# Decayed keys of six blocks turned by DMA instead of TensorE, in a linear-attention kernel followed by a dense layer

## The chip, the cores and the metric

One core of a Trainium2 chip runs the whole program. The metric is the device time in microseconds of one execution. Before the change three runs took 573.35, 575.41 and 577.69 us, median 575.41 us.

## The reference

An RWKV-6 attention over batch 4, 8 heads, 768 tokens and head size 48, and then a dense layer whose activation is h - tanh(h):

```
for t in range(S):
    cur = einsum('bhd,bhe->bhde', u * k_t, v_t)
    y_t = einsum('bhd,bhde->bhe', r_t, state + cur)
    state = w_t[..., None] * state + einsum('bhd,bhe->bhde', k_t, v_t)
x = y as [3072, 384]
h = x @ w_in            # [3072, 2048]
out = (h - tanh(h)) @ w_out
```

All inputs and outputs are 32-bit floats.

## The kernel before, in words

The work is cut into eight blocks: 4 batches times 2 halves of 384 tokens. Block 0's attention is computed first (`boot`). Then the loop `for i, blk in enumerate(blocks)` runs the dense layer of block i in 16 steps (`f` from 0 to 15, 128 columns of the hidden layer each), and between the steps, on the same engines, the attention of the next block (`later`, block i+1) and the first preparations of the one after it (`after`, block i+2). "Step 7 of block 4" below means f = 7 in the loop for i = 4. Every engine's order of instructions is written out by hand (`manual_schedule`) and is the order in which the program emits them; an engine whose next instruction has to wait holds up everything behind it. SP issues nearly all DMAs, in one queue.

**A step of the dense layer.** TensorE (PE) makes `hp` by three matmuls (L720) into a single PSUM buffer, so the next step's `hp` can only start when ScalarE has copied this one to `h` (L723). From block 2 on ScalarE then does three more passes of 384 (L741, L742, L744), VectorE (DVE) makes `g` from them one step later (L726), and then forms sums of pieces of `g` (L767), which PE multiplies two steps later (L835): in these "fast" blocks the second product is done in pairs of steps with fewer products of 128x128. In blocks 0 and 1 the second product is the plain one (L797). A block takes about 66 us.

**The attention of the next block.** A tile holds two pairs of heads in each half (`HALVES` = pairs 2, 3 and pairs 0, 1; `UP` = 2); partitions are head dimensions, columns are tokens. DVE scans the decays `w` from behind into the tile `post` (`behind`, L387) and from the front into `pre` (`before`, L376), and multiplies keys into `post` (`times_behind`, L401) and r into `pre` (`times_before`, L394). `bound` (L418, ScalarE) reads `w` for a check. Then PE works through phases, each put at a step by `plan(i)`:

- `earlier`: products of `post` and `pre` (L447), copied under a mask by DVE (L454);
- `turn`: `post` has to be had with tokens on the partitions. PE transposes 12 pieces of 128x128 (L471) into two PSUM scratch tiles, and ScalarE copies them into the tile `ks` (L473, two copies of 768);
- `update`: PE multiplies `ks` with `v` (L496); one step later DVE chains the products into the states (`update_2`, L508 and L518, eleven or twelve instructions);
- `result 1` and `result 2`: PE multiplies states (L561) and scores (L578); ScalarE copies the result to `xT`, the input of the next block's dense layer.

Other DVE work of the next block, on keys and r with tokens on the partitions: `product_u` (L343), `product_r` (L347), `product_sum` (L351), `diagonal_in` (L358). The two token tables are loaded at steps 3 and 4 (L339; at 4 and 5 in block 1), into the tiles `k` and `r`; `w`, `k` and `r` of the block after are loaded at steps 7, 9 and 11 (L330) into the same tiles, each of which has one buffer. `post`, `w` and `ks` have one buffer too.

Of the kernel before, what the change touches and what calls it, by code (L numbers as in the profile page):

```python
# [42 lines left out]
U16 = mybir.dt.uint16  # L43
# [8 lines left out]
P = 128  # L52
L = 64
NB = 384
NQ = S // NB
NCH = NB // L
NCP = NCH // 2
# [3 lines left out]
HALF = WIDE // 2 + 2  # L61
UP = 2
# [58 lines left out]
def kernel(  # L121
# [12 lines left out]
    nc = tc.nc  # L134
# [29 lines left out]
    start = const.tile([P, UP * NCH * LP], F32, name="start", tag="start")  # L164
# [116 lines left out]
    class Block:  # L281
# [183 lines left out]
        def turn(self, ps, p0, ahead=0):  # L465
# [6 lines left out]
                                        self.chunk("post", p0 + p, 2 * c, n=2), ident)  # L472
            nc.scalar.copy(out=ks.rearrange("t p c d -> t p (c d)"), in_=tp[:, :, 0:NCP * P])  # L473

        def keys(self):
            if not hasattr(self, "ks"):
                self.ks = work.tile([P, NPAIR, NCP, P], F32, name="ks", tag="ks", bufs=1)
            return self.ks
# [142 lines left out]
        def phase(self, ps, name):  # L621

            if name in ("own", "earlier"):
                return [getattr(self, name)(ps, p0) for p0 in HALVES]
            if name == "turn":
                for p0 in HALVES:
                    self.turn(ps, p0)
            elif name == "update":
                self.update_1(ps)
                return [self.update_2]  # L630
            elif name == "result 1":
                self.results(ps)
                self.result("from_states", ALL)
            elif name == "result 2":
                self.result("from_scores", ALL, True)
                self.result_out(ALL)
                self.fill_holes([nc.sync])
            return []
# [247 lines left out]
    def plan(i):  # L886


        converted = ()
        if i == 0:  # L890
            phases = {4: "turn", 6: "update", 8: "own", 11: "earlier", 13: "result 1"}
            before = {0: ("behind 2", "take_whole 2"), 1: ("behind 0", "take_whole 0", "times_behind 2"),
                      2: ("times_behind 0",), 3: ("before 2",), 4: ("times_u 2",), 5: ("before 0", "times_u 0"),
                      8: ("times_before", "held", "bound 2"), 9: ("bound 0",)}
            ahead = {}
            converted = range(READY + 1, NF)
            loads = {f: "weights" for f in (0, 1, 3, 4, 5, 6, 7, 8, 9, 10)}
            loads.update({2: "next r", 11: "w", 12: "k", 13: "r"})
        else:
            phases = {4: "earlier", 7: "turn", 10: "update", 12: "result 1"}  # L900
            before = {0: ("times_behind 2",), 1: ("times_behind 0",), 3: ("times_before", "held"), 4: ("bound 2",),
                      5: ("product_u",), 6: ("bound 0", "product_r"), 7: ("product_sum",), 8: ("diagonal_in 2",),
                      9: ("diagonal_in 0",)}
            if i == 1:
                phases = {6: "earlier", 8: "turn", 10: "update", 12: "result 1"}
                before.update({0: ("behind 2", "take_whole 2"), 1: ("behind 0", "take_whole 0"),
                               2: ("before 2", "times_behind 2"), 3: ("before 0", "times_behind 0"),
                               4: ("times_before", "held", "bound 2")})
            ahead = {10: ("behind 2", "take_whole 2"), 12: ("behind 0", "take_whole 0"), 13: ("before 2",),
                     15: ("before 0",)}  # L910
            loads = {1: "v", 3 + (i == 1): "tokens k", 4 + (i == 1): "tokens r", 7: "w", 9: "k", 11: "r"}
        return phases, before, ahead, converted, loads

# [94 lines left out]
    ps_a = mains.enter_context(tc.tile_pool(name="ps_a", bufs=2, space=PSUM))  # L1008
    acc = [ps_d.tile([P, BANK], F32, name=f"acc{j}", tag=f"acc{j}") for j in range(NB // P)]
    count = const.tile([P, 1], F32, name="count", tag="count")  # L1010
    ahead_of_h, rest, formed, extra, behind, due, summed = [], [], [], [], [], [], []
# [14 lines left out]
    for i, blk in enumerate(blocks):  # L1026
        here = xT
        later = blocks[i + 1] if i + 1 < len(blocks) else None
# [13 lines left out]
        for f in range(NF):  # L1042
            now = i * NF + f
            for op in ahead_of_h:
                op()
            if i == 0 and f in (1, 2):
                busy(acc[0], 2)
            h, made = first(here, f, ps_d)
            g, ahead_of_h, square, later_ops = slight(h, now, i, f)
            for op in rest + behind + square + formed + extra:  # L1050
                op()
            rest, behind, formed = later_ops, [], []
            if not now:
                for op in fourth[0]:
                    op()
                extra = fourth[1]
            if f + READY in converted:
                ops, extra = convert(*raws.pop(0))
                for op in ops:
                    op()  # L1060
            elif f:
                extra = []
            if f < few[i]:
                q = f // 2
                formed = [form_g(q, n) for n in (range(2, len(G_FORMS), 2) if f % 2 else (0,))]
                if f % 2:
                    due += [(now + 2, fewer.add, (q, 0)), (now + 2 + (f + 1 < few[i] or second is None), fewer.add, (q, 1))]
            else:
                due.append((now + LAG + (not later), second.add, (f, g)))
            if fewer and f == 9:  # L1070
                fewer.others(ps_a, range(4))
            if fewer and second:
                if f == 2 * LAST + 1:
                    fewer.others(ps_a, range(4, LAST))
                    behind.append(fewer.others_summed)
                elif f in (2 * LAST + 2, 2 * LAST + 3):
                    fewer.sum(*((0, 6) if f % 2 == 0 else (6, len(SUMS))))
                elif f == 2 * LAST + 4:
                    second.rows = fewer.gathered()
            if not later and f == NF - 2:  # L1080
                at = n_whole + n_excess
                nc.vector.tensor_single_scalar(holds[:, n_whole:at], excess, 0.0, op=ALU.is_le)
                sum_held(holds[:, at:at + n_top - 2], top[:, 0:n_top - 2], holds[:, 0:at + n_top - 2], ends[:, 0:1])
            if later:
                for name in before.get(f, ()):
                    later.prepare(name)
                if f in phases:
                    behind += later.phase(ps_a, phases[f])
            if after:
                for name in ahead.get(f, ()):  # L1090
                    after.prepare(name)
            if fast and i == 1 and f >= 4 and f - 4 < len(W_FORMS):
                form_w(f - 4, 0)
            for n in {1: {4: (0,), 8: (1,), 14: (2, 3)},
                      2: {0: (4,), 1: (5,), 2: (6, 7), 4: (8,), 6: (9,)}}.get(i, {}).get(f, ()) if fast else ():
                form_w(n, 4)
            some = ({4: (0, 2), 6: (2, 4), 8: (4, 6), 9: (6, 8), 14: (8, len(SUMS))} if later else
                    {4: (0, 4), 6: (4, 8), 8: (8, len(SUMS))}).get(f)
            if some and summed:
                summed[0].sum(*some)  # L1100
                if some[1] == len(SUMS):
                    summed.pop().store()
            name, ins = loads.get(f), None
            if name == "weights":
                ins = more_weights(nc.sync)
            elif name and name.startswith("tokens"):
                ins = later.load_tokens(name[-1]) if later else None
            elif name == "v":
                ins = later.load_v() if later else None
            elif name and name != "next r" and after:  # L1110
                ins = after.load(name)
            if name == "next r":
                ins = later.load("r")
            if ins:
                begin_behind(made, ins)
            if i == 0 and f == 3:
                later.load_v()
            if i == 0 and f == 6:
                nc.sync.dma_start(out=u_row, in_=u_all)
            if f < 2 and summed:  # L1120
                summed[0].others(ps_a, ((4, 5, 6), (7,))[f])
                if f:
                    behind.append(summed[0].others_summed)
            while due and due[0][0] <= now:
                _, add, what = due.pop(0)
                add(*what)
            if later and phases.get(f) == "result 1":
                behind += later.phase(ps_a, "result 2")
        if fewer and later:
            summed.append(fewer)  # L1130
# [79 lines left out]
```

## Time and profile before

| | us |
|---|---|
| median of three runs | 575.41 |
| span of the profiled execution | 572.0 |
| busy: PE / DVE / ACT | 553.3 / 477.7 / 345.3 |
| one block (2 to 6) | about 66.2 |
| one step without attention work, blocks 2 to 6 | 3.28 |
| in a block of 66.2 us (333.0 to 399.2): PE / DVE / ACT busy | 66.09 / 59.55 / 42.62 |

The span runs from the first to the last instruction on the core; the device time includes what lies around it. Busy times come from one execution and count an instruction from its start to its end; matmuls overlap in the array, so the time that a matmul takes from PE is read from the start of one to the start of the next. The granted TensorE clock was full (1.00) in all blocks.

Starts of ScalarE's copy to `h` in block 4, which mark the steps:

| step | 3 | 4 | 5 | 6 | 7 | 8 | 9 | 10 | 11 |
|---|---|---|---|---|---|---|---|---|---|
| us | 315.57 | 318.85 | 323.88 | 327.15 | 330.43 | 335.02 | 338.29 | 344.25 | 349.26 |

Step 4 holds `earlier`, step 7 the turn, step 9 an extra set of products for the second layer, step 10 the update.

### The profile page before, as it was taken

To read this page: it belongs to the slowest core of one execution; us is meant where nothing else is said; L and a number is where in the kernel's file an instruction comes from. 1 tells how busy PE (TensorE), PEld (TensorE's weight loads), DVE (VectorE), ACT (ScalarE), POOL (GpSimd) and SP (SyncE) were. 2 spreads that over 40 slices of the span, in tenths; PEclk is the share of its full clock that TensorE was granted. 3 is DMA by queue.
4 is the path that set the end of the run, shared out by engine and by line. 5 is a ranking of instruction groups with operands and counts; after the bars stand their busy time and mean duration, and the time that the engine had idled before them with its cause. 6 is when DMAs were issued, how large, how long until landed. Compare 5 with 4: busy or idle time off the path is not lost.

```text
span 572.0 us, 14041 instructions
## 1 busy us (share of the span) xinstructions
PE 553.3 (97%) x5736; PEld 404.7 (71%) x5736; DVE 477.7 (84%) x926; ACT 345.3 (60%) x702; POOL 11.9 (2%) x40
## 2 busy tenths in 40 slices
PE   4889999999999999999999999999999999999996
PEld 4646666566665887777778787777878777787763
DVE  8878884799879989889998989989998998658673
ACT  3979893343137755577566775767556775667441
POOL 6100000000000000000000000000000000000000
PEclk9999999999999999999999999999999999999999
DMA  8496553222203232041212231122221300100101
GB/s 323 174 333 208 180 181 109 83 84 76 92 11 107 69 105 64 5 125 57 74 62 72 84 113 57 53 84 85 72 66 49 120 2 2 44 10 1 41 2 45
DMA packets 32453, 50.40 MB, mean 88 GB/s; under 512 B 2560, under 2 KB 30336, under 8 KB 32384
## 3 DMA queue, kind: packets, MB, share of 16 engines
q1 hardware_dynamic: 32144, 49.38, 26.9%
q8 instruction: 46, 0.75, 0.6%
q14 instruction: 23, 0.19, 0.1%
q0 software_dynamic: 96, 0.07, 0.1%
q10 hardware_dynamic: 144, 0.00, 0.0%
HBM read 43.55 MB, written 4.72 MB: 84 GB/s over the span
## 4 chain that ended last, share of the span: by engine, by line
PE 92%; ACT 2%; DVE 2%; DMA 2%; issue 1%; SPq 0%; DVEq 0%
PE hp L720 42%; PE acc L835 22%; PE acc L797 13%; PE att L835 5%; PE att L447 2%; PE att L471 2%; PE att L561 2%; PE att L496 2%; PE att L578 2%; ACT up L255 1%; DMA r<-in_rT 1%; DMA w<-in_wT 1%; DVE post L387 1%; DVE post L401 0%; ACT w_sb L255 0%
## 5 line engine op out<-in xcount | busy, mean ns | idle before, releaser
L720 PE MATMUL hp<-xT,w_sb 128*128 128x384 f32 x768 | 270.1, 488 | 2.0 <-ACT h L723 1.4
L720 PEld LDWEIGHTS hp<-xT,w_sb 128*128 128x128 f32 x768 | 138.4, 190 | 81.7 <-ACT h L723 4.4
L723 ACT ACTIVATE h<-hp 128x384 f32<-128x384 f32 x128 | 62.6, 489 | 150.2 <-PE hp L720 148.5
L835 PE MATMUL acc<-forms,g 128*128 128x128 f32 x810 | 121.1, 277 | 0.5
L835 PEld LDWEIGHTS acc<-forms,g 128*128 128x128 f32 x810 | 108.7, 192 | 15.6 <-issue 1.2
L767 DVE TENSOR_TENSOR g<-g 128x256 f32<-128x256 f32 x225 | 95.5, 424 | 19.8 <-DVE g L767 0.9
L726 DVE SCALAR_TENSOR_TENSOR h<-h,s 128x384 f32<-128x384 f32 x128 | 70.5, 550 | 10.6 <-ACT s L741 9.9
L797 PE MATMUL acc<-w_sb,sums 128*128 128x384 f32 x192 | 68.1, 491 | 1.6 <-DVE sums L726 1.3
L726 DVE SCALAR_TENSOR_TENSOR g<-qa,h 128x384 f32<-128x384 f32 x96 | 53.6, 558 | 17.1 <-PE acc L835 4.0
L742 ACT ACTIVATE qa<-s,shift 128x384 f32<-128x384 f32 x90 | 55.4, 615 | 2.9
L744 ACT ACTIVATE junk<-s,shift 128x384 bf16<-128x384 f32 x90 | 53.9, 599 | 0.0
L797 PEld LDWEIGHTS acc<-w_sb,sums 128*128 128x128 f32 x192 | 35.6, 190 | 25.9 <-DVE sums L726 2.6
L741 ACT ACTIVATE s<-h 128x384 f32<-128x384 f32 x90 | 47.1, 523 | 2.9
L835 PE MATMUL acc<-w_sb,g 128*128 128x128 f32 x270 | 44.9, 275 | 0.0
L752 ACT ACTIVATE qa<-s,shift 128x384 f32<-128x384 f32 x38 | 23.2, 611 | 24.7 <-DVE top L749 24.7
L835 PEld LDWEIGHTS acc<-w_sb,g 128*128 128x128 f32 x270 | 37.4, 192 | 0.0
L749 DVE CUSTOM_DVE_ANT_0 s<-h 128x384 f32<-128x384 f32 x38 | 21.0, 553 | 12.8 <-ACT h L723 12.8
L255 ACT ACTIVATE up<-raw 128x768 f16<-128x768 f32 (+1 forms) x32 | 31.7, 1056 | 0.0
L726 DVE SCALAR_TENSOR_TENSOR sums<-qa,h 128x384 f32<-128x384 f32 x32 | 17.9, 558 | 15.6 <-ACT qa L752 12.2
L835 PE MATMUL att<-w_sb,g 128*128 128x128 f32 x180 | 30.2, 275 | 0.0
L835 PEld LDWEIGHTS att<-w_sb,g 128*128 128x128 f32 x180 | 26.4, 192 | 4.5
L387 DVE TENSOR_TENSOR_SCAN post<-w,seed 128x780 f32<-128x780 f32 x16 | 28.5, 1784 | 1.1 <-DMA w<-in_wT 1.0
(87 smaller groups left out, 529.1 us busy)
## 6 DMA issues: line engine op xcount, KB each, us to landing
raw<-in_weights SPq DMA_DIRECT2D x16, 768.0 KB, 4.4
w<-in_wT SPq DMA_DIRECT2D x7, 780.0 KB, 4.6
k<-in_kT SPq DMA_DIRECT2D x7, 768.0 KB, 4.7
r<-in_rT SPq DMA_DIRECT2D x7, 768.0 KB, 4.5
v_sb<-in_v SPq DMA_DIRECT2D x8, 576.0 KB, 4.2
k<-in_tokens SPq DMA_DIRECT2D x6, 576.0 KB, 3.9
r<-in_tokens SPq DMA_DIRECT2D x6, 576.0 KB, 4.0
out_y<-sums SPq DMA_DIRECT2D x15, 128.0 KB, 1.9
```

The source lines that it names most:

```text
L255: return lambda: nc.scalar.activation(out=to, in_=of, func=AF.Copy, scale=scale, bias=bias)
L387: return nc.vector.tensor_tensor_scan(out=back(t[:, 0:width]), data0=back(self.tile("w")[:, a:a + width]), data1=back(seed[:, 0:width]), i ...
L720: nc.tensor.matmul(hp, lhsT=w_in_sb[:, f, kc, :], rhs=xT[kc], start=(kc == KC - 1), stop=(kc == 0))
L723: return h, nc.scalar.activation(out=h, in_=hp, func=AF.Copy, scale=1.0 / UPSCALE)
L726: return lambda: nc.vector.scalar_tensor_tensor(out=out, in0=in0, scalar=scalar, in1=in1, op0=op0, op1=ALU.mult)
L741: nc.scalar.activation(out=s, in_=h, func=AF.Square)
L742: nc.scalar.activation(out=qa, in_=s, func=AF.Square, bias=shift[:, 4:5])
L744: nc.scalar.activation(out=junk[:, 0:NB], in_=s, func=AF.Relu, bias=shift[:, 5:6], accum_out=excess[:, at:at + 1])
L752: first = [lambda: nc.scalar.activation(out=qa, in_=s, func=AF.Square, bias=shift[:, 4:5])]
L767: return lambda: nc.vector.tensor_tensor(out=G[:, to:to + 2], in0=two(G, g_at(q, a0), g_at(q, a1)), in1=two(G, g_at(q, b0), g_at(q, b1)), ...
L797: nc.tensor.matmul(acc, lhsT=g[:, j * P:(j + 1) * P], rhs=w_out_sb[:, f, :], start=(f == self.first), stop=(f == NF - 1))
L835: nc.tensor.matmul(to, lhsT=G[:, g_at(q, a), :], rhs=rhs, start=start, stop=stop, skip_group_check=True)
```

## The change

The transposes on PE (`turn`) stay for the first two blocks (in `boot`, and in the loop for i = 0). For the other six, computed in the loops i = 1 to 6, they are replaced by DMA transposes, which move 16-bit words. A 32-bit word is therefore split into its low and its high half:

- `split` (ScalarE): the 768 columns of half of `post` are copied as 16-bit words, every second word, into two planes of 768 words each, in the tile `w`, whose decays are no longer needed. In block 1 one copy does both planes (1536 words); later the first half of `post` goes in two copies of 768, the second in one of 1536.
- `turned` (SP): one DMA transpose of 128 x 1536 16-bit words, 12 pieces of 128 columns. The one for pairs 2, 3 writes the first half of `ks`, the one for pairs 0, 1 the first half of `post`, after `earlier` has read it.
- `join` (ScalarE): copies of 512 words (one chunk pair, two head pairs, two planes) into every second 16-bit word of `ks`; three for each half.

```diff
+        def turning(self, p0):
+            def at(name, start):
+                return self.tile(name)[:, start:start + UP * NB].bitcast(U16)
+            if p0:
+                return at("w", HALF + 2), self.keys()[:, 0:UP].rearrange("t p c d -> t (p c d)").bitcast(U16)
+            return at("w", 0), at("post", 0)
+
+        def split(self, p0, planes):
+            src = self.tokens("post", p0, UP).bitcast(U16).rearrange("d (t two) -> d two t", two=2)
+            dst = self.turning(p0)[0].rearrange("d (two t) -> d two t", two=2)
+            nc.scalar.copy(out=dst[:, planes], in_=src[:, planes])
+
+        def turned(self, p0):
+            words, turned = self.turning(p0)
+            nc.sync.dma_start_transpose(out=turned.rearrange("t (n d) -> t n d", d=P), in_=words)
+
+        def join(self, p0, cs):
+            dst = self.keys()[:, p0:p0 + UP].bitcast(U16).rearrange("t p c (d two) -> t c two p d", two=2)
+            src = self.turning(p0)[1].rearrange("t (two p c d) -> t c two p d", two=2, p=UP, c=NCP)
+            for c in cs:
+                nc.scalar.copy(out=dst[:, c], in_=src[:, c])
...
         else:
-            phases = {4: "earlier", 7: "turn", 10: "update", 12: "result 1"}
-            before = {0: ("times_behind 2",), 1: ("times_behind 0",), 3: ("times_before", "held"), 4: ("bound 2",),
-                      5: ("product_u",), 6: ("bound 0", "product_r"), 7: ("product_sum",), 8: ("diagonal_in 2",),
+            phases = {3: ("split 2 0",), 4: ("earlier", "split 2 1", "turned 2", "split 0 01"), 5: ("turned 0",),
+                      6: ("join 2 0",), 7: ("join 2 1",), 8: ("join 2 2",), 9: ("join 0 02",), 10: ("update",),
+                      12: ("result 1",)}
+            before = {0: ("times_behind 2",), 1: ("times_behind 0",), 3: ("times_before", "held"),
+                      5: ("product_u",), 6: ("product_r",), 7: ("product_sum",), 8: ("diagonal_in 2",),
                       9: ("diagonal_in 0",)}
             if i == 1:
-                phases = {6: "earlier", 8: "turn", 10: "update", 12: "result 1"}
+                phases.update({3: (), 4: ("split 2 01", "turned 2"), 5: ("split 0 01",), 6: ("earlier", "turned 0"),
+                               7: ("join 2 02",), 8: ()})
                 before.update({0: ("behind 2", "take_whole 2"), 1: ("behind 0", "take_whole 0"),
-                               2: ("before 2", "times_behind 2"), 3: ("before 0", "times_behind 0"),
-                               4: ("times_before", "held", "bound 2")})
-            ahead = {10: ("behind 2", "take_whole 2"), 12: ("behind 0", "take_whole 0"), 13: ("before 2",),
-                     15: ("before 0",)}
+                               2: ("before 2", "times_behind 2"), 3: ("bound 2", "before 0", "times_behind 0"),
+                               4: ("bound 0", "times_before", "held")})
+            ahead = {10: ("behind 2", "take_whole 2", "bound 2", "bound 0"), 12: ("behind 0", "take_whole 0"),
+                     13: ("before 2",), 15: ("before 0",)}
```

In `plan`, "split 2 01" means planes 0 and 1 of the half that begins with pair 2; "join 0 02" means the pieces 0 to 2 of the half that begins with pair 0. In each engine's order this takes 72 transposes off PE, adds the copies on ScalarE and two DMAs per block on SP, and moves the two `bound`s of a block ahead, to step 10 of the loop before, since `split` writes over `w`. DVE's instructions and their order are the same as before. On SP the first transpose of a block comes between the loads of the k tokens and of the r tokens (in block 1 ahead of both), the second between the r tokens and the load of `w`.

More of the change, by code (lines that the diff above doesn't have):

```diff
@@ L627, in phase @@
                     self.turn(ps, p0)
+            elif name.startswith(("split", "turned", "join")):
+                what, p0, *part = name.split()
+                getattr(self, what)(int(p0), *(slice(int(x[0]), int(x[-1]) + 1) if what == "split" else
+                                               range(int(x[0]), int(x[-1]) + 1) for x in part))
             elif name == "update":
@@ L890, in plan @@
         if i == 0:
-            phases = {4: "turn", 6: "update", 8: "own", 11: "earlier", 13: "result 1"}
+            phases = {4: ("turn",), 6: ("update",), 8: ("own",), 11: ("earlier",), 13: ("result 1",)}
             before = {0: ("behind 2", "take_whole 2"), 1: ("behind 0", "take_whole 0", "times_behind 2"),
@@ L1086 @@
                     later.prepare(name)
-                if f in phases:
-                    behind += later.phase(ps_a, phases[f])
+                for name in phases.get(f, ()):
+                    behind += later.phase(ps_a, name)
             if after:
@@ L1126 @@
                 add(*what)
-            if later and phases.get(f) == "result 1":
+            if later and "result 1" in phases.get(f, ()):
                 behind += later.phase(ps_a, "result 2")
```

## The prediction

> **What bounds the kernel now.** I read the page first: the engines' shares and the chain of waits.
>
> ```profile
> span 572.0 us, 14041 instructions
> PE 553.3 (97%) x5736; PEld 404.7 (71%) x5736; DVE 477.7 (84%) x926; ACT 345.3 (60%) x702; POOL 11.9 (2%) x40
> PE 92%; ACT 2%; DVE 2%; DMA 2%; issue 1%; SPq 0%; DVEq 0%
> ```
>
> The end is set by TensorE, whose queue hardly ever waits: the waits of PE between 184 and 531 us are an empty list. So work taken off PE counts, as long as the engines that feed it keep up. PE's own order of time in block 5 gives the price of a turn (start, duration, then what):
>
> ```profile
> 394.47 2.10 PE L720 MATMUL hp<-xT,w_sb 128*128 128x384 f32 x6
> 396.41 1.47 PE L471 MATMUL att<-ident,post 128*128 128x128 f32 x12
> 397.72 1.06 PE L835 MATMUL acc<-forms,g 128*128 128x128 f32 x8
> ```
>
> Twelve transposes hold PE from 396.41 to 397.72: 1.31 us. Next, DVE's waits, in three windows of one block each (266.9 to 333, 333 to 399.2, 399.2 to 465.5 us; total, times, longest):
>
> ```profile
> DVE g L726 <- PE acc L835: 0.3, 1, 0.3
> DVE h L726 <- ACT s L741: 0.2, 1, 0.2
> ...
> DVE g L767 <- PE att L447: 0.5, 1, 0.5
> DVE g L767 <- DVE g L767: 0.5, 1, 0.5
> ...
> DVE g L726 <- PE acc L835: 0.2, 1, 0.2
> ```
>
> VectorE is as full as PE there: it waits 0.5, 1.0 and 0.2 us in 66 us. The same view gives 3.2 us in the window before and 10.5 in the one after. Last, ScalarE in step 3 of block 4, and the DMA issues (KB each, us to landing):
>
> ```profile
> 315.57 0.49 ACT L723 ACTIVATE h<-hp 128x384 f32<-128x384 f32 x1
> 316.10 0.52 ACT L741 ACTIVATE s<-h 128x384 f32<-128x384 f32 x1
> 316.65 0.62 ACT L742 ACTIVATE qa<-s,shift 128x384 f32<-128x384 f32 x1
> 317.18 0.60 ACT L744 ACTIVATE junk<-s,shift 128x384 bf16<-128x384 f32 x1
> 317.68 0.19 ACT L744 ACTIVATION_READ_ACCUMULATOR junk<-s,shift 128x1 f32 x1
> 318.85 0.49 ACT L723 ACTIVATE h<-hp 128x384 f32<-128x384 f32 x1 [0.98 <-PE hp L720]
> ```
>
> ```profile
> r<-in_tokens SPq DMA_DIRECT2D x6, 576.0 KB, 4.0
> ...
> out_y<-sums SPq DMA_DIRECT2D x15, 64.0 KB, 1.6
> ...
> r<-in_rT SPq DMA_DIRECT2D x2, 384.0 KB, 6.2
> ```
>
> A step costs ScalarE 2.3 us (315.57 to 317.87) of 3.28, and 0.98 is left.
>
> **Removed: PE's turn.** 6 blocks x 1.31 = 7.9 us, all on the path. The two scratch tiles it took in PSUM free nothing, as PE waited for none. ScalarE loses two copies of 768 (1.48 us) a block, and two bounds of 1.13 us move to step 10 of the block before.
>
> **Added on ScalarE.** A block (2 to 6) gets two splits of 768, one of 1536 and six joins of 512. Rows: a copy of 768 from PSUM 0.74 (half of 1.48), a conversion of 768 to 16 bits 0.95 (two in 1.90), 512 from PSUM 0.53 (two in 1.06). I take 0.8, 1.45 and 0.55, nearest the copies; the upper ends are 0.95, 1.9 and 0.66. Each step has a budget, from one h of block 4 to the next: step 3: 2.3+0.8 = 3.1 of 3.28; step 4: 2.3+0.8+1.45 = 4.55 of 5.03 (318.85 to 323.88; 5.15 at the upper ends); steps 6 to 8: 2.85 of 3.28; step 9: its scaling copy ends 3.17 after h, plus 1.65 = 4.8 of 5.96; step 10: 2.3+2.26 = 4.6 of 5.01. PE also bears an h that is 0.65 late (h of step 5 ends 324.37, the next hp starts 325.02). So ScalarE costs 0 at both ends. The cover is this slack; without it each us late in h is a us of PE.
>
> **Added on SP's queue and ScalarE's: the transposes.** None is in the trace. Each moves 128x1536 16-bit words, 384 KB. Lower bound: between the rows of 64 KB (1.6) and 576 KB (4.0), 384 KB come to 3.1 us; the nearest slow row of that size is 6.2 (a load queued behind others at the start). A far upper bound is twelve pieces of 128 columns one by one at the shortest landing, 12 x 1.6 = 19 us. I take 3.1, the row of its size and issue. The Trainium skill, page Advanced Engine Details and Errata, section X-Bar Transpose (TRN2), says such transposes run as fast as ordinary DMAs. No run here shows that yet; it would leave the sum as it is.
>
> What waits for them, in block 4. The first is issued when split 2 1 ends: 318.85+2.3+0.8 = 321.95. The join at step 6 stands at 327.15+2.3 = 329.45, so it may take 7.5 us; behind it on ScalarE are all later h. Behind it on SP is the load of the r tokens, before issued at 319.37 and now at 321.95 or later. If it runs behind the transpose, it lands at 321.95+3.1+2.7 (its 4.0 less the fixed 1.3) = 327.75. Its reader L347 starts at 328.60: 0.85 us to spare, cost 0. The load of w waits for both transposes to have read that tile; it was issued at 330.95, landed by 335.6 and is read at 345.31: 9.7 to spare, cost 0. The second transpose is read at step 9, 13 us later.
>
> In block 1 the k tokens also fall behind a transpose. Before: issued 118.18, read by L343 at 124.26. Now split 2 01 ends at 117.51+0.52+1.13+1.45 = 120.6, and the load lands at 124.6 (beside the transpose) to 126.4 (behind it): DVE is 0.4 to 2.1 us late, once. It idles 1.2 us at 140 to 144 before its states are due at 153. I take 0.4, between 0 and 0.8.
>
> **What is late next: DVE.** Its order and work are unchanged, yet PE now wants it 1.31 us sooner per block. The window after the turn of block 2 has 3.2 us idle and pays. The next three have 0.5, 1.0 and 0.2 and fall short by 0.8+0.3+1.1 = 2.2 us. Against that stands DVE's lead. The tightest place is the states: in block 4 the last product ends at 352.62, and PE's group L561, started at 352.43 over 1.63 us in six chunks, reads it about 1.3 us on: 1.1 to spare. So 1.1 to 2.2 of it reaches PE; I take 1.5, as other blocks have 1.7 to 2 to spare.
>
> **Sum.** 7.9 - 1.5 - 0.4 = 6.0 us: span 572.0 to 566.0. The runs of before scatter from 573.35 to 577.69, median 575.41, 3.4 above the profiled span; the forecast is 575.4 - 6.0 = 569.4 us, its own range 567.5 to 572.
>
> **Rivals.**
> 1. *All 7.9 us are kept*: DVE's lead absorbs the shortfall; its forms end 2 to 5 us before PE reads them. Against it: the states' 1.1. 575.4-7.9 = 567.5 us. Chance 0.11.
> 2. *The transposes are slow and starve DVE* (slower than before). Place: r tokens behind the first transpose, then L347 and the whole of DVE behind it, in five blocks. Spare 0.85, so from 3.95 us per transpose each us costs 5 us; from 5.15 us (3.95 + 6.0/5) the gain is gone. At the 6.2 row: 2.25 x 5 = 11.3, 569.4+11.3 = 580.7 us. At 8 us: 20.3, 589.7 us. For it: 16-bit pieces scattered over partitions are like no row here; DVE has nothing to spare. Against: 384 KB is small, and one instruction issues it. The Trainium skill, VectorE: DVE Perf Modes, section The three transpose paths, puts a DMA transpose of 128x128 bf16 at 1309 ns, against 390 ns on TensorE; twelve in a row would be an estimated 15.7 us and 628 us in all. Chance 0.24.
> 3. *16-bit strided copies cost ScalarE double*: 1.6, 2.9, 1.1. Step 4 then ends 7.4-5.03 = 2.4 late (0.6 of it from step 3), less 0.65 borne = 1.7 of PE, with 0.2 in the others 1.9 a block, 9.5 in five: 579 us. For it: no such row. Against: 16-bit conversions with a stride cost 0.95. Chance 0.10.
>
> **How the numbers follow.** The forecast has 0.55. About 1%, 5.8 us, is what a measurement tells from no change, and 6.0 lies at that edge: 0.33 of the 0.55 is beyond it. Faster: 0.33+0.11 = 0.44. Within 1%: 0.22 + 0.08 (transposes of 4.5 to 6 us) + 0.06 of rival 3 = 0.36. Slower: 0.16+0.04 = 0.20. The range runs from 567 to 581: rival 1 and rival 2 up to the 6.2 row are in; some 0.14 of slower transposes, 0.03 of rival 3 and 0.02 below are out.
>
> **What would show it.** L471 falls from 96 transposes to 24. The r tokens land before L347, without a wait on DMA there. DVE's waits in the windows above go to about 0, while PE begins to wait for the states at L561, 0.3 to 1 us a block. ACT's h stays within 0.65 us of hp. A step of 3.28 us that grows at steps 5 to 7, with DVE or ACT waiting on a DMA, would make the forecast wrong by rival 2; h late at step 5 without such a wait, by rival 3.

## The result, and the profile after

| | median us | runs |
|---|---|---|
| before | 573.99 (573.02 to 578.16) | 20 |
| changed | 572.37 (569.57 to 575.14) | 20 |

The ratio is 0.9959 (95% interval 0.9940 to 0.9978): a gain of 0.2 to 0.6%, within 1%. The forecast, 569.4 of 575.4, was a ratio of 0.9895.

The spans, 572.0 before and 572.4 after, show none of this gain: `boot` lasted 4.3 us longer in the profiled execution of the changed kernel (its first `hp` starts at 32.24 against 27.90 us). The granted clock was 0.50 there from 24.8 to 31.7 us, and 1.00 in the trace of before; the same kernel run again later, with 1.00, had its first `hp` at 27.91. In that later comparison the executions with a mean granted clock of 0.998 or more have medians of 573.81 us (8 of before) and 570.65 us (5 of the changed kernel), 3.2 us apart. From here on "six blocks" means the time from the first `hp` of block 1 to the first `hp` of block 7, all that the change touches. It is a sharp measure: the changed kernel, run again later, gave 396.50 after 396.51 us (single blocks differed by up to 0.26 us).

| six blocks, us | block 1 | 2 | 3 | 4 | 5 | 6 | sum |
|---|---|---|---|---|---|---|---|
| before | 70.37 | 64.48 | 66.19 | 66.18 | 66.31 | 66.18 | 399.71 |
| changed | 71.19 | 62.88 | 65.74 | 65.75 | 66.08 | 64.87 | 396.51 |
| difference | +0.82 | -1.60 | -0.44 | -0.43 | -0.24 | -1.31 | -3.20 |

The page of the changed kernel, its spans, engines and chain of waits:

```profile
span 572.4 us, 13965 instructions
PE 548.7 (96%) x5664; PEld 398.9 (70%) x5664; DVE 477.5 (83%) x926; ACT 376.8 (66%) x743; POOL 11.9 (2%) x40
PE 74%; DVE 19%; issue 3%; DMA 2%; ACT 1%; DVEq 0%; SPq 0%; ACTq 0%
```

PE lost 72 matmuls and 4.6 us of busy time, ScalarE gained 31.5 us, and DVE now holds 19% of the chain, where it held 2%. The order of time on PE in block 5 (start, duration, what) shows the turn gone:

```profile
396.03 2.10 PE L749 MATMUL hp<-xT,w_sb 128*128 128x384 f32 x6
397.96 1.05 PE L864 MATMUL acc<-forms,g 128*128 128x128 f32 x8
398.86 0.39 PE L864 MATMUL acc<-w_sb,g 128*128 128x128 f32 x2
399.08 0.39 PE L864 MATMUL acc<-forms,g 128*128 128x128 f32 x2
399.30 2.10 PE L749 MATMUL hp<-xT,w_sb 128*128 128x384 f32 x6
```

Nothing stands between the step's `hp` and its second product, and the step takes 399.30 - 396.03 = 3.27 us, like one without attention work. Step 7 is 1.31 us shorter in each of blocks 2 to 6, and there every other step but step 12 keeps its length to 0.01 us. So why is the sum not 7.9? The waits of PE between 184 and 532 us, an empty list before (total, times, longest; L586 is the L561 of before, L543 its L518):

```profile
PE att L586 <- DVE states L543: 1.9, 3, 0.9
PE hp L749 <- ACT h L752: 0.6, 1, 0.6
```

The second row is not new: it is 0.58 us at step 3 of block 2, and the kernel before has the same wait at 180.7 us, just ahead of this window. In blocks 3, 4 and 5 step 12 is 0.87, 0.89 and 1.07 us longer than before: 2.83 of the gain is handed back there. DVE meanwhile hardly waits. Its list of waits for the 66 us from the middle of block 3 to the middle of block 4 (268.0 to 333.7) has one row; that of the next 66 us is empty:

```profile
DVE g L755 <- PE acc L864: 0.2, 1, 0.2
```

The list before held 0.5 and 1.0 us there: DVE was nearly full and is now full. (In block 4 it is busy for 59.76 of 65.75 us, and what is left are gaps below 0.15 us from one instruction to the next, besides one wait of 0.2.) What exactly PE waits for at step 12 shows in block 4, PE first and then DVE:

```profile
353.24 0.33 PE L586 MATMUL att<-pre,states 48*64 48x64 f32 x4
354.02 1.61 PE L586 MATMUL att<-pre,states 48*64 48x64 f32 x92 [0.45 <-DVE states L543]
```

```profile
346.95 1.78 DVE L387 TENSOR_TENSOR_SCAN post<-w,seed 128x780 f32<-128x780 f32 x1
348.76 0.17 DVE L407 TENSOR_SCALAR whole<-post 128x12 f32<-128x12 f32 x1
...
353.52 0.35 DVE L543 TENSOR_TENSOR states<-states,att 128x192 f32<-128x192 f32 x1
353.91 0.36 DVE L533 TENSOR_TENSOR states<-states,whole 128x192 f32<-128x192 f32 x1
```

Four passes, two matmuls, start, and then PE stands until 354.02. At that time the last product (L533) is still running, until 353.91 + 0.36 = 354.27, so PE waits for something earlier: the last addition (L543), which ends at 353.52 + 0.35 = 353.87. This addition reads the second of the two PSUM scratch tiles (`att`), and the third matmul of `result 1`, the first one for the odd pairs, writes into that tile again. So the last addition, not the last product, is what PE needs first, and it needs it almost at once. In the three other blocks that wait, the third matmul starts 0.14 to 0.15 us after the last addition ends, too (157.09 to 157.24 in block 1, 288.13 to 288.27 in block 3, 419.96 to 420.10 in block 5). The same place of block 4 in the trace of before:

```profile
352.43 1.63 PE L561 MATMUL att<-pre,states 48*64 48x64 f32 x96
351.88 0.35 DVE L518 TENSOR_TENSOR states<-states,att 128x192 f32<-128x192 f32 x1
352.26 0.36 DVE L508 TENSOR_TENSOR states<-states,whole 128x192 f32<-128x192 f32 x1
```

There the third matmul began at 286.35, 352.53 and 418.78 in blocks 3, 4 and 5, and the last additions ended at 285.70, 352.23 and 418.64. Less those 0.15 us, the spare was 0.5, 0.15 and 0 us.

The other loss is block 1. DVE there, and SP's queue (start, duration, what):

```profile
127.47 0.08 DVE L778 DVE_READ_ACCUMULATOR2_ANT top<- 128x1 f32 x1
130.31 1.36 DVE L343 TENSOR_TENSOR k<-k,u_row 128x1152 f32<-128x1152 f32 x1 [2.76 <-DMA k<-in_tokens]
```

```profile
123.52 1.56 SPq L492 DMA_TRANSPOSE ks<-w  x1
125.21 0.81 SPq L339 DMA_DIRECT2D k<-in_tokens  x1
126.14 0.43 SPq L339 DMA_DIRECT2D r<-in_tokens  x1
```

The load of the k tokens stands behind the transpose and DVE waits 2.76 us for it, where before it waited for no DMA in that stretch. Block 1 keeps nothing of its 1.31 and adds 0.82: 2.13 lost. With the 0.29 us that step 12 of block 2 became shorter (why is open), the account closes: 6 x 1.31 - 2.83 - 2.13 + 0.29 = 3.2.

ScalarE in step 3 of block 4 with its first split, and the DMA issues (us to landing at the end):

```profile
319.67 0.19 ACT L773 ACTIVATION_READ_ACCUMULATOR junk<-s,shift 128x1 f32 x1
319.76 0.81 ACT L488 COPY w<-post 128x768 uint16<-128x768 uint16 x1
320.83 0.49 ACT L752 ACTIVATE h<-hp 128x384 f32<-128x384 f32 x1 [0.26 <-PE hp L749]
```

```profile
r<-in_tokens SPq DMA_DIRECT2D x6, 576.0 KB, 4.9
...
ks<-w SPq DMA_TRANSPOSE x6, 3.7
post<-w SPq DMA_TRANSPOSE x6, 5.3
```

The split fits into the 0.98 us that step 3 had left and leaves 0.26. The first transpose of a block lands 3.7 us after its issue, the second 5.3 (it runs while the r tokens are loaded; in the run further down in which they are loaded behind it, it took 4.0).

### The profile page after: what moved, and what is told of

It is laid out like the page before. It is cut to its first block, busy times and chain, and to the rows that moved or that the text cites. A ratio compares the mean times of both kernels' runs of the same rounds, so it can differ in the third digit from the quotient of the medians.

```text
span 572.4 us, 13965 instructions
## 1 busy us (share of the span) xinstructions
PE 548.7 (96%) x5664; PEld 398.9 (70%) x5664; DVE 477.5 (83%) x926; ACT 376.8 (66%) x743; POOL 11.9 (2%) x40
## 4 chain that ended last, share of the span: by engine, by line
PE 74%; DVE 19%; issue 3%; DMA 2%; ACT 1%; DVEq 0%; SPq 0%; ACTq 0%
PE hp L749 34%; PE acc L864 18%; PE acc L826 9%; PE att L864 4%; PE att L447 2%; PE att L586 2%; DVE g L796 2%; PE att L603 2%; DVE h L755 2%; DVE post L387 2%; DVE g L755 1%; DVE states L543 1%; DVE states L533 1%; DVE scores L358 1%; DMA r<-in_rT 1%
## 5 line engine op out<-in xcount | busy, mean ns | idle before, releaser
L376 DVE TENSOR_TENSOR_SCAN pre<-w,start 128x780 f32<-128x780 f32 x16 | 28.5, 1783 | 0.6
```

Of the source, the lines that this page charges most:

```text
L376: return nc.vector.tensor_tensor_scan(out=self.tile("pre")[:, cols], data0=self.tile("w")[:, cols], data1=start[:, 0:n * NCH * LP], initia ...
```

## The experiments

Theory A: the missing gain is DVE's, at two places, the states at step 12 (blocks 3 to 5) and the k tokens in block 1; PE and ScalarE have nothing to do with it. Rivals: ScalarE's joins and splits delay PE; the transposes delay everything behind them; some cost spreads over all steps.

**The scan behind the states.** The look-ahead scan (L387 at 346.95 above) and its `take_whole` are 1.95 us of DVE work right in front of the states. They move one step later.

```diff
-            ahead = {10: ("behind 2", "take_whole 2", "bound 2", "bound 0"), 12: ("behind 0", "take_whole 0"),
+            ahead = {10: ("bound 2", "bound 0"), 11: ("behind 2", "take_whole 2"), 12: ("behind 0", "take_whole 0"),
```

> Only the order on DVE changes: the scan 'behind' for pairs 2, 3 (about 1.95 us with its maximum) moves from step 10 to step 11, behind the chain of states. Theory A (the missing part is DVE's: PE waits at step 12 for the last add of the states, since the second tile of results takes the PSUM buffer that this add reads): the chain ends 1.9 us sooner, the waits of 0.87, 0.89 and 1.07 us in step 12 of blocks 3 to 5 go, and up to 1.4 us in block 1: 2.8 to 4 us less than the changed kernel. Theory B (the missing part is spread: DMA transposes disturb PE or the clock): step 12 keeps its length, 0 us.

**The loads ahead of the transpose.** The first transpose is issued at step 5, behind both token loads (in block 1 behind the k tokens alone; there the r tokens still follow it).

```diff
-            phases = {3: ("split 2 0",), 4: ("earlier", "split 2 1", "turned 2", "split 0 01"), 5: ("turned 0",),
+            phases = {3: ("split 2 0",), 4: ("earlier", "split 2 1", "split 0 01"), 5: ("turned 2", "turned 0"),
...
-                phases.update({3: (), 4: ("split 2 01", "turned 2"), 5: ("split 0 01",), 6: ("earlier", "turned 0"),
+                phases.update({3: (), 4: ("split 2 01",), 5: ("turned 2", "split 0 01"), 6: ("earlier", "turned 0"),
```

> The first transpose of each block is put at step 5 instead of 4, so that the k tokens (block 1) and the r tokens (all blocks) go ahead of it on SP; nothing else changes. Theory A with the queue in block 1: the wait of 2.8 us of L343 for the k tokens goes, the step in block 1 where PE waits for the states shrinks by 1.4 us and the step of the former turn gives its 1.31 in full: about 2 us less than the changed kernel, and nothing in blocks 2 to 6, where the r tokens landed 0.2 to 0.7 us before their reader. Theory B: 0 us.

**Both edits.**

> Both edits together. Theory A: the parts add up, 4.6 to 5 us less than the changed kernel, and all six blocks give 1.31 us: 7.9 us below the kernel before, 566 us. If another of DVE's results becomes late instead (the sums of g at step 15, which had 1.8 to 2.1 us to spare), 1 to 2 us less gain than that. Theory B: 0 us.

**One piece of DVE work taken out.** `product_u` (L343), 1.36 us of DVE, is left out of the six blocks, with its wait for the k tokens.

```diff
-                      5: ("product_u",), 6: ("product_r",), 7: ("product_sum",), 8: ("diagonal_in 2",),
+                      6: ("product_r",), 7: ("product_sum",), 8: ("diagonal_in 2",),
```

> The multiplication of the keys by u (L343, 1.35 us of DVE at step 5 of blocks 1 to 6) is left out, so the diagonal terms of the output lack u. Theory A: DVE reaches the states 1.35 us sooner, which is more than the 0.87 to 1.07 us of PE's waits: 2.8 us less than the changed kernel, plus up to 1.4 us in block 1. Theory B, or a wait that comes from PE's own side: 0 us.

Measured, five rounds on one chip, and the six blocks of each profile (a "-" is within 0.3 us of the changed kernel):

| | median us | ratio to before (95%) | six blocks | block 1 | 3 | 4 | 5 | 6 |
|---|---|---|---|---|---|---|---|---|
| scan behind states | 568.42 | 0.9888 (0.9858 to 0.9918) | 394.13 | -1.14 | -0.78 | -0.88 | -0.38 | +0.79 |
| loads ahead | 569.20 | 0.9896 (0.9869 to 0.9922) | 394.32 | -2.13 | - | - | - | - |
| both | 568.67 | 0.9899 (0.9865 to 0.9934) | 393.14 | -2.13 | -0.78 | -0.86 | -0.38 | +0.79 |
| without `product_u` | 569.31 | 0.9906 (0.9876 to 0.9936) | 393.32 | -2.13 | -0.28 | -0.20 | -0.57 | - |

The medians of the four can't be told apart; the six blocks can. *Loads ahead* gave back the 2.13 us of block 1 whole, so that loss was the place of the load and nothing else. *Scan behind states* removed the wait in blocks 3 and 4 and in block 1 (1.39 of step 12; 0.25 of it came back at step 8), and gave 2.4 where 2.8 to 4 was expected, because DVE, which has no slack left, is late elsewhere. The waits of PE between 184 and 532 us with the scan moved:

```profile
PE hp L749 <- ACT h L752: 0.6, 1, 0.6
PE att L586 <- DVE states L543: 0.5, 2, 0.3
PE att L447 <- DVE holds L423: 0.4, 2, 0.2
```

The states' 1.9 became 0.5: the waits of blocks 3 and 4 are gone, that of block 5 fell from 0.92 to 0.25, and block 6 has a new one of 0.28. And a new row has come: `earlier` (L447) waits for `held` at step 4, the work that the moved scan pushes back. It costs 0.29 and 0.23 us in blocks 5 and 6, and step 12 of block 6, free in the changed kernel, now costs 0.56. *Both* took off 3.4 us where 4.6 to 5 was expected. In each block it has the larger of the two gains, not their sum: the 1.14 of block 1 that the moved scan won is part of the 2.13 that the loads win there, and in blocks 3 to 6 it has what the moved scan had. *Without `product_u`* gave back the 2.13 of block 1 but only 1.05 us in blocks 3 to 5, where 2.8 was expected: a DVE that is 1.36 us earlier came to the next token product (L347) as its data landed, waited for DMA and for ScalarE's `s` instead, and lost much of its lead.

**Again, and the last wait.** The changed kernel and both edits once more, on another chip, and `product_u` left out with the loads ahead.

> The changed kernel as it is, beside the next one on the same chip: 0.4% below the kernel before, about 572 us; the six blocks from the first hp of block 1 to that of block 7 take 396.5 us again.

> The order with the states first and the loads first, on the same chip as the changed kernel: its six blocks took 393.1 us in one profile against 396.5, so 3.4 us less. If the gain of that order was a matter of the chip or of the launch, less than 1 us.

> The multiplication by u is left out of the diagonal terms again, and the loads of the tokens go ahead of the first transpose. Leaving it out alone freed 1.35 us of DVE, but step 12 gave back only 0.2 to 0.6 us in blocks 3 to 5, with DVE reaching L347 as the r tokens landed. Theory D (the late r tokens stood right behind DVE's lag and took its place): with the load ahead the rest comes, step 12 gives 0.9 to 1.1 us in each of these blocks against the changed kernel, and the six blocks take 391.5 to 393 us. If the rest was held by something else, they take 393.3 us as before.

| | median us | ratio to before (95%) | six blocks |
|---|---|---|---|
| changed | 571.95 | 0.9950 (0.9927 to 0.9972) | 396.50 |
| both edits | 568.73 | 0.9882 (0.9846 to 0.9918) | 393.18 |
| no `product_u`, loads ahead | 567.54 (one run) | | 392.68 |

On the same chip both edits take 3.2 us off the changed kernel in the medians and 3.3 in the six blocks: this version beats both kernels. The third gave 0.46, 0.45 and 0.80 us in blocks 3 to 5 beyond the changed kernel, some 60% of what step 12 had lost. PE's list of waits between 184 and 532 us, which counts from 0.15 us, is empty here. Still, in blocks 3, 4 and 5 the third matmul of `result 1` starts at 282.90, 348.20 and 413.48, again 0.14 to 0.15 us after the last addition (282.75, 348.05, 413.34), and in block 4 before the last product ends (348.44). It is the same wait, smaller: 0.41, 0.44 and 0.28 us of step 12. Whether still less DVE work ahead of step 9 would end it wasn't tried; the waits speak against it. Over blocks 2 to 6 DVE waited 11.4 us for ScalarE's `s` here, where the changed kernel waits 8.5, so 2.9 of the 6.8 us won at step 5 (five times 1.36) went into that wait, and from step 9's `g` to the states of block 4 (338.60 to 348.05) DVE works without a pause.

**The second rival priced.** In blocks 2 to 6 the r tokens are loaded one step later, behind the second transpose, so that they land as late as slower transposes would have made them.

```diff
-            loads = {1: "v", 3 + (i == 1): "tokens k", 4 + (i == 1): "tokens r", 7: "w", 9: "k", 11: "r"}
+            loads = {1: "v", 3 + (i == 1): "tokens k", 5: "tokens r", 7: "w", 9: "k", 11: "r"}
```

> The load of the r tokens moves behind the second transpose (step 5) in blocks 2 to 6. It then lands 1 to 2 us after DVE wants it, where before 0.2 to 0.7 us ahead. Theory: DVE has nothing to spare in blocks 3 to 5, so each us late is a us of PE there and is partly taken up in blocks 2 and 6: 4 to 8 us more than the changed kernel, with DVE waiting at L347. If DVE's lag hides it: under 1 us.

It took 581.08 us, and the six blocks grew by 10.2 to 406.73 us (+0.74, +2.59, +4.30, +2.45, +0.18 in blocks 2 to 6), all of it at step 12. DVE's waits between 184 and 532 us hold the cause:

```profile
DVE k L347 <- DMA r<-in_tokens: 5.4, 5, 1.2
```

So the rival's place was right: from this point, late r tokens reach PE through the states. But 5.4 us of waits made 10.2, above the 4 to 8 expected. In block 4 PE waited 1.32 and 0.45 us and then ran slowly:

```profile
354.45 0.33 PE L586 MATMUL att<-pre,states 48*64 48x64 f32 x4 [1.32 <-DVE states L543]
355.24 2.56 PE L586 MATMUL att<-pre,states 48*64 48x64 f32 x92 [0.45 <-DVE states L543]
357.88 1.22 PE L864 MATMUL acc<-forms,g 128*128 128x128 f32 x4
```

and the busy times by stretch have the granted clock in the column behind POOL (then the DMA share and GB/s):

```profile
352.00:354.40 2.40, 1.13 (x4) 0.38 (x2) 2.19 (x7) 1.35 (x5) 0.00 (x0) 1.00 0.88 305
354.40:358.00 3.60, 3.01 (x97) 2.75 (x97) 3.22 (x8) 1.06 (x3) 0.00 (x0) 0.67 0.02 5
358.00:362.00 4.00, 4.00 (x60) 3.78 (x64) 3.69 (x6) 0.00 (x0) 0.00 (x0) 0.50 0.00 0
362.00:366.00 4.00, 4.00 (x75) 3.13 (x68) 2.40 (x4) 2.36 (x6) 0.00 (x0) 0.95 0.06 16
```

The clock fell to half for several us; the other 92 passes took 2.56 us, not 1.61, and four passes of the second product 1.22, not 0.71. Some 3 of the block's 4.3 us are this. In blocks 3 and 5 it is 1.5 and 1.6 us: 6.1 of the 10.2 come behind the waits, at the lower clock, and 4.1 from the waits themselves.

**ScalarE's slack.** Each join copy is made twice.

```diff
             for c in cs:
-                nc.scalar.copy(out=dst[:, c], in_=src[:, c])
+                for _ in range(2):
+                    nc.scalar.copy(out=dst[:, c], in_=src[:, c])
```

> Each of the three copies that join the planes on ScalarE is made twice, in all six blocks: about 2 us more of ScalarE work a block (three copies took 2.01 us in the changed kernel's trace). Theory: ScalarE has slack, so the joins cost nothing where they stand; the doubled ones delay the chunk-one steps by part of their 2 us only, +2 to +6 us over the six blocks (396.5 becomes 398.5 to 402.5). Rival: ScalarE is already on the path with the joins as they are; then every doubled copy is paid in full and six blocks grow by 12 us or more.

The expectation counted three joins a block; there are six, so 36 copies were added, and ScalarE's busy time rose from 376.8 to 400.1 us. The six blocks grew by 1.87 us, to 398.38: below either theory's figures, and far below 23. Where it went shows how the two limits stand side by side: steps 8 to 10 became 1.0 us longer in blocks 2 to 6 (0.85 of it at step 10, where `update` waits for the joins), but step 12 of blocks 3, 4 and 5 became 0.87, 0.76 and 1.20 us shorter. In blocks 2 and 6, where no wait for the states hides it, the doubled copies cost 1.01 us each. A PE that is 1 us late at step 10 finds its states ready at step 12. In those blocks the end is set by DVE's states, whatever PE does ahead of them.

**The control: the same move in the kernel before.**

```diff
-            ahead = {10: ("behind 2", "take_whole 2"), 12: ("behind 0", "take_whole 0"), 13: ("before 2",),
+            ahead = {11: ("behind 2", "take_whole 2"), 12: ("behind 0", "take_whole 0"), 13: ("before 2",),
```

> The kernel before with the second look-ahead piece behind the block's states instead of ahead of them, the same move that gave the changed kernel 2.4 us. Theory A: before, the states came with 0 to 0.5 us to spare at step 12, so there is little to win: six blocks stay within 0.5 us of 399.7. Rival: the move is worth the same in any kernel, whatever turns the keys; then six blocks fall by about 2 us.

The six blocks went from 399.71 to 399.60 us; only block 5 moved, by 0.13. The states were just in time before; they became late when PE came 1.31 us sooner.

## Why the prediction was nearly right, by its steps

- **PE's turn, 6 x 1.31 = 7.9 us.** Right, to the hundredth: with the loads ahead of the transpose block 1, too, keeps exactly 1.31.
- **ScalarE, 0.** Right. The copies took 0.81, 1.47 and 0.75 us (two joins in a row 0.62 apart), where 0.8, 1.45 and 0.55 were taken; the join is over its upper end of 0.66, and the slack covered it. PE's one wait for `h` between 184 and 532 us is there before the change too, and another 23 us of copies cost 1.87. Rival 3, copies at double the price, is out.
- **The transposes, 3.1 us.** Too short: 3.7, and 5.3 for the second. With 0.85 us of spare for the r tokens it was close. In block 4 they landed at 330.37, and L347, at the same place in its block as before, began at 330.59: 0.2 us were left (0.2 to 0.7 in the five blocks). That this term stayed at 0 was in part luck. Rival 2 named 3.95 us as its point of no return; the measured 3.7 stayed on the right side, and the late r tokens showed that it would have cost more than was said, since the clock joins in. As to the Trainium skill: VectorE: DVE Perf Modes, section The three transpose paths, with 1309 ns for each 128x128, would give an estimated 15.7 us for twelve in a row, against 3.7 here for all twelve pieces of one instruction; Advanced Engine Details and Errata, section X-Bar Transpose (TRN2), as fast as ordinary DMAs, is nearer, though not quite met: 384 KB in 3.7 us, where the plain rows of this case gave an estimated 3.1 for that size.
- **Block 1's k tokens, 0.4 us.** This step failed in size: 2.13. It took the load to run beside the transpose. SP's queue was held 1.69 us by the transpose (123.52 to the next issue at 125.21), and the load then landed 5.0 us after its issue: in the time of before, at 127.0, beyond the later of its two bounds, 126.4.
- **DVE's states, 1.5 us.** The mechanism was right, and so were the place and blocks 3 to 5; the size was 2.83. The step that failed is the spare of 1.1 us: it was read from the last product and the chunk of matmuls that reads it, but PE's third matmul needs the PSUM tile that the last addition reads, which left 0 to 0.5 us; the 1.7 to 2 us given to other blocks were 0.5 and 0 in blocks 3 and 5. The shortfall, 0.8 + 0.3 + 1.1 = 2.2 us from DVE's idle times, was near; no spare was to be had against it. The sign that was named came: PE waits for the states there, 0.58, 0.45 and 0.92 us in blocks 3 to 5. With the two edits, 393.14 is 6.6 us under before, about what had been forecast for the change as it was.

The sum was 6.0 and the six blocks gained 3.2, about half: the places of all losses were named, and two sizes were too small. The medians, 573.99 and 572.37, differ by 1.6; their interval holds 1.3 to 3.4 us. So the outcome with 0.36, within 1%, came, and not the one with 0.44. That 572.37 lies only 3 us above the forecast time is in part luck: the forecast was reckoned from 575.41, and the kernel before now has a median 1.4 us lower. Rival 1, all kept, fell with the 2.83.

## What to carry over

When a full engine gives work away, look at every wait that its next neighbour meets only just in time. "Just in time" is measured to the first thing that the consumer needs, and that can be a buffer it writes, not the data it reads. And a DMA put into a shared queue has to be counted at each load behind it, block by block: here the load of one block lost a quarter of what all six had to win.

## What the runs showed of the hardware

- **A transposing DMA holds its queue.** Its issue on SP took 1.47 and 1.45 us for 128x1536 16-bit words, against 0.37 for a plain load of the k tokens (block 4), and the transposes of six blocks brought the DMA packets under 512 bytes from 2,560 to 21,376.
- **The clock fell after short waits of PE, three times of three at one place.** With the r tokens late, step 12 of blocks 3, 4 and 5 had two waits of 1.62, 1.77 and 1.72 us in all, and each time the granted clock fell to 0.50 behind them (287.4 to 290.7, 355.7 to 362.3 and 427.3 to 430.6 us); waits of 1.10 us and less at the same place in the changed kernel left it at 1.00. The Trainium skill, page TensorE: Matmul & The Clock Gate, section What's actually happening, names an idle window of about 3.4 us; here 1.6 to 1.8 us, in two pieces around two small matmuls, were followed by it. But the length of the wait alone does not decide: without `product_u` and with the loads ahead, PE waited 2.06 us in one piece in `boot` (until 29.43), and the clock stayed at 1.00. What else has a part in it, the DMA traffic for one, wasn't tried.
